# Another order of steps and loads in a chunked attention with a multiplicative feed-forward, and a last output block in four pieces

## The chip, the cores and the metric

The kernel runs on one core of a Trainium2 chip, in one launch. The metric is the device time of the core in microseconds (us). Five engines work side by side, each through its own list of instructions in order: TensorE (PE) multiplies, VectorE (DVE) and ScalarE (ACT) work on what it leaves in PSUM, GpSimd (POOL) issues the loads, and SyncE (SP) issues moves and stores.

## The reference

```python
q, k, v: (8, 8, 576, 64)          # batch, heads, sequence, head_dim
# chunks of 64 along the sequence, each chunk attends to itself alone
scores = q_c @ k_c.T / 8
attn   = softmax(scores)
out    = attn @ v_c
x      = out as (4608, 512)       # tokens x (heads * head_dim)
a = x @ w1; b = x @ w2            # 512 -> 1024
h = (a * b) @ w3                  # 1024 -> 1024
y = h @ w_out                     # 1024 -> 512, float32
```

All inputs are float32 in memory. The kernel works in bfloat16 and accumulates in float32.

## The kernel before, in words

The 4608 tokens are 18 *pairs* p = 0 to 17 of 256 tokens (four chunks with all eight heads); two pairs make one of nine *groups* g of 512 tokens. The two last products are folded: w3 @ w_out is computed once on the chip (`w3o`), so that each token is multiplied by w1, w2 and then by `w3o`.

Nothing is scheduled by loops. The string `ORDER` lists every step by a letter with its indices, and a loop at the end of `first_path` calls `do[letter](indices)`. The order of the steps in the string is the order of the instructions on each engine; between engines they run as their semaphores allow. The letters:

- Loads by POOL (queue q0, with a cast from float32 to bfloat16; one *block* is 256 KB as it lands): `q5`, `k5`, `v5` are q, k and v of pair 5 (each one block, in one to three DMAs); `i0` to `i3` are quarters of w1 and w2; `h0` and `h1` are the halves of w3 (four DMAs of one block each), `o` is w_out (four of one block). At most eight of POOL's DMAs are outstanding: each one's issue waits for the landing of the eighth before it. A q also waits until the transpose that read its buffer five pairs earlier is through, a v until the P that read its buffer six pairs earlier is.
- The first pair goes another way (`R`, `K`, and `D` for products with zeros while nothing else is there).
- `T5.0`, `T5.1` (DVE, L207): the 32x32 transposes of q and of k of pair 5. `G3.0`, `G3.1` (SP, four moves each): for pairs from 6 on, the transposed q and k of a group are moved to other partitions.
- `S5` (PE): scores; `E5` (ACT, L240): exponential; `P5` (PE): times v, with a column of ones for the sum. `N5.0`, `N5.1` (DVE, L269 and L272): reciprocal and normalization of the two halves of the tokens; each frees a PSUM buffer of P5.
- `X5.0`, `X5.1` (DVE, L305 or L313): transposes of the normalized x. `H3.0`, `H3.1` (SP, four moves each): the moves that follow for pairs from 6 on.
- `A6.2`, `B6.2` (PE): x times w1 and w2, a part of 128 (pairs below 4: 256) columns of d_ff; `C6.2` (ACT, L370) copies A's product from PSUM, `M6.2` (DVE, L387) multiplies it with B's. Pairs 0 to 3 go one by one; from pair 4 on, the steps of an even p cover a whole group of 512 tokens.
- `V0` to `V7` (DVE, L428): transposes of parts of w3; `W0` to `W3` (PE): w3 @ w_out; `Z0` to `Z3` (ACT): `w3o` from PSUM. W0 needs V0, V1 and all of w_out; V0 to V3 need h0, V4 to V7 need h1; W2 needs V4 and V5, W3 needs V6 and V7.
- `O5` (PE): the output of pair 5, from `w3o`; `Y5` (ACT, L417): from PSUM to SBUF; `Q5` (SP): its store, 512 KB.

All of PSUM is four buffers of two banks, and S, each half of P, A with B, W and O all take one. So a step of PE also waits for the reader of some earlier product: for an E, an N, an M, a Z or a Y. Which one is fixed when the program is built; the prediction names those that matter.

The last output, `O17`, goes in pieces, so that the copies and stores begin earlier: rows 0 to 127 in one piece of 512 columns, rows 128 to 255 in pieces of fewer columns, each with its own PSUM buffer, copy and store (L403 to L411).

Of the kernel before, what the change touches and what calls it, by code (L numbers as in the profile page):

```python
# [7 lines left out]

ORDER = """
R0.0 R1.0 R0.1 R1.1 v0 D0.0.1.9.512 K0.0 K1.0 T0.0.0 K0.1 T0.1.0 K1.1 S0.0 T0.0.1 E0.0 T0.1.1 q1 k1  # L10
S0.1 i0 E0.1 P0.0 T1.0 P0.1 D0.1.0.6.512 v1 N0.0 T1.1 N0.1 X0.0 X0.1 i1 S1 E1 D1.0.0.6.512 A0.0 B0.0
C0.0 i2 P1 q2 A0.1 B0.1 N1.0 k2 N1.1 C0.1 X1.0 i3 A0.2 C0.2 X1.1 A1.0 M0.0 M0.1 v2 q3 A1.1 B0.2 B1.0
B1.1 T2.0 k3 T2.1 v3 C1.0 M0.2 C1.1 S2 E2 q4 k4 A0.3 M1.0 M1.1 B0.3 P2 h0 o C0.3 M0.3 A1.2 N2.0 N2.1
X2.0 X2.1 T3.0 B1.2 A1.3 B1.3 C1.2 A2.0 C1.3 T3.1 C2.0 B2.0 M1.2 M1.3 S3 A2.1 E3 B2.1 P3 T4.0 M2.0
N3.0 C2.1 N3.1 A2.2 X3.0 C2.2 X3.1 B2.2 q5 h1 A2.3 B2.3 A3.0 M2.1 M2.2 v4 B3.0 A3.1 A3.2 V0 C2.3
M2.3 T4.1 C3.0 B3.1 k5 B3.2 V1 M3.0 W0 C3.1 q6 q7 k6 Z0 V2 q8 S4 V3 C3.2 k7 M3.1 W1 T5.0 v5 V4 E4 V5
V6 V7 W2 W3 T5.1 Z1 Z2 A3.3 T6.0 k8 q9 k9 Z3 M3.2 S5 T6.1 T7.0 q10 T7.1 E5 v6 v7 C3.3 P4 B3.3 N4.0
X4.0 M3.3 O0 G3.0 N4.1 k10 Y0 G3.1 T8.0 O1 X4.1 P5 T8.1 Y1 O2 Q0 N5.0 N5.1 X5.0 v8 X5.1 A4.0 S6 E6
T9.0 T9.1 S7 B4.0 T10.0 Y2 q11 O3 C4.0 M4.0 Q1 E7 P6 v9 N6.0 A4.1 N6.1 C4.1 Y3 B4.1 A4.2 X6.0 M4.1
G4.0 A4.3 X6.1 C4.2 P7 N7.0 C4.3 B4.2 G4.1 k11 B4.3 N7.1 X7.0 A4.4 M4.2 B4.4 Q2 M4.3 C4.4 T10.1 M4.4  # L20
A4.5 C4.5 S8 B4.5 A4.6 C4.6 A4.7 E8 B4.6 Q3 C4.7 X7.1 B4.7 M4.5 q12 P8 H3.0 M4.6 S9 H3.1 M4.7 O4 E9
T11.0 Y4 P9 N8.0 O5 k12 N8.1 A6.0 B6.0 Y5 T11.1 G5.0 T12.0 A6.1 X8.0 N9.0 B6.1 C6.0 C6.1 T12.1 A6.2
q13 X8.1 B6.2 N9.1 X9.0 M6.0 k13 C6.2 v10 T13.0 v11 X9.1 M6.1 A6.3 M6.2 q14 G5.1 C6.3 A6.4 q15 B6.3
C6.4 B6.4 A6.5 S10 C6.5 B6.5 T13.1 M6.3 M6.4 A6.6 H4.0 E10 P10 H4.1 M6.5 S11 N10.0 B6.6 k14 N10.1
v12 A6.7 C6.6 E11 G6.0 P11 M6.6 N11.0 B6.7 X10.0 N11.1 A8.0 A8.1 B8.0 G6.1 C6.7 C8.0 B8.1 A8.2 B8.2
C8.1 M6.7 T14.0 q16 A8.3 M8.0 C8.2 M8.1 X10.1 M8.2 X11.0 Q4 q17 T14.1 H5.0 B8.3 C8.3 S12 S13 X11.1
A8.4 E12 C8.4 B8.4 k15 H5.1 M8.3 E13 v13 k16 A8.5 B8.5 P12 M8.4 k17 v14 T15.0 N12.0 N12.1 O6 A8.6
v15 C8.5 C8.6 T15.1 Y6 T16.0 B8.6 A8.7 M8.5 C8.7 P13 Q5 M8.6 B8.7 X12.0 A10.0 C10.0 B10.0 N13.0
N13.1 M8.7 G7.0 A10.1 T16.1 C10.1 A10.2 X12.1 X13.0 M10.0 C10.2 G7.1 B10.1 B10.2 A10.3 B10.3 C10.3
M10.1 T17.0 A10.4 C10.4 M10.2 M10.3 A10.5 T17.1 B10.4 M10.4 X13.1 v16 H6.0 S14 C10.5 S15 G8.0 B10.5  # L30
M10.5 O7 G8.1 E14 E15 P14 A10.6 H6.1 N14.0 C10.6 B10.6 A10.7 N14.1 Q6 Y7 M10.6 P15 N15.0 N15.1 C10.7
X14.0 S16 B10.7 M10.7 O8 E16 Q7 A12.0 B12.0 C12.0 M12.0 Y8 A12.1 C12.1 P16 S17 N16.0 X14.1 B12.1 E17
A12.2 M12.1 B12.2 A12.3 C12.2 A12.4 B12.3 X15.0 B12.4 v17 C12.3 M12.2 A12.5 N16.1 B12.5 M12.3 H7.0
X15.1 A12.6 X16.0 A12.7 C12.4 M12.4 C12.5 M12.5 C12.6 P17 N17.0 Q8 B12.6 B12.7 M12.6 H7.1 A14.0
A14.1 C12.7 B14.0 N17.1 C14.0 M12.7 O9 B14.1 C14.1 Y9 A14.2 X16.1 M14.0 M14.1 C14.2 A14.3 B14.2 Q9
O10 B14.3 X17.0 H8.0 Y10 Q10 A14.4 C14.3 A14.5 X17.1 C14.4 B14.4 M14.2 B14.5 H8.1 M14.3 A14.6 O11
Y11 B14.6 M14.4 O12 C14.5 C14.6 Y12 A14.7 M14.5 A16.0 C14.7 C16.0 Q11 M14.6 B14.7 A16.1 C16.1 A16.2
B16.0 B16.1 M14.7 M16.0 C16.2 M16.1 Q12 A16.3 O13 B16.2 B16.3 A16.4 C16.3 M16.2 Y13 M16.3 C16.4
A16.5 A16.6 B16.4 A16.7 C16.5 B16.5 M16.4 O14 Y14 C16.6 B16.6 C16.7 M16.5 B16.7 M16.6 Q13 M16.7 O15
Y15 O16 Q14 Q15 Y16 Q16 O17  # L40
"""


# [5 lines left out]
def first_path(  # L49
# [11 lines left out]
    nc = tc.nc  # L61
    B, H, S, D = q.shape
    P = 128
# [5 lines left out]
    DM = H * D  # L69
# [22 lines left out]
    def inorder(ins):  # L92
        tc.keep_in_program_order(ins)
        return ins
# [7 lines left out]
    def psum(name):  # L102
        return ps.tile([P, 2, 512], f32, tag="p", name=name)
# [285 lines left out]
    def store(p, u0, u1, n0, n1, o_sb):  # L389
        move(out[p * PT + u0 * UT:p * PT + u1 * UT, n0:n1].rearrange("(u p) n -> p u n", p=UT), o_sb)  # L390

    def mm_o(dst, p, u, n0, n1):
        for ki in range(FO):
            t0 = p % 2 * PT + u * UT
            mm(dst, lhsT=ab_t[p // 2][:, ki, t0:t0 + UT],
               rhs=w3o[:, ki, n0:n1], start=(ki == 0), stop=(ki == FO - 1))

    def do_O(p):
        if p < NP - 1:
            ps_t[p] = psum("o_ps")  # L400
            for u in range(2):
                mm_o(ps_t[p][:, u, :], p, u, 0, DM)
            return  # L403

        o_sb = msb.tile([P, 2, DM], f32, tag="o_sb", name="o_sb")
        for u, n0, n1, copy in ((0, 0, DM, nc.scalar.copy), (1, 0, DM - P, nc.scalar.copy),
                                (1, DM - P, DM, nc.vector.tensor_copy)):
            t = psum("o_ps")
            mm_o(t[:, 0, 0:n1 - n0], p, u, n0, n1)
            inorder(copy(o_sb[:, u, n0:n1], t[:, 0, 0:n1 - n0]))  # L410
            store(p, u, u + 1, n0, n1, o_sb[:, u:u + 1, n0:n1])  # L411
# [42 lines left out]
    def load_half3(i):  # L454
# [10 lines left out]
    do = {"q": load_q, "k": load_k, "v": load_v, "i": load_w12, "o": load_wo, "h": load_half3, "T": do_T, "S": do_S, "R": do_R, "K": do_K, "E": do_E, "w": do_w, "x": do_x, "G": do_G, "H": do_H,  # L465
          "P": do_P, "N": do_N, "X": do_X, "A": do_A, "B": do_B, "C": do_C, "M": do_M, "D": do_D, "V": do_V,
          "W": do_W, "Z": do_Z, "O": do_O, "Y": do_Y, "Q": do_Q}
    for step in ORDER.split():
        do[step[0]](*(int(n) for n in step[1:].split(".") if n))
# [119 lines left out]
```

## Time and profile before

| | |
|---|---|
| median of 3 runs | 241.62 us (241.2 to 242.22) |
| the profiled execution | 242.34 us |
| its span (first to last instruction) | 240.8 us |
| mean granted TensorE clock | 0.993 |
| TensorE busy | 229.8 us (95%) |
| DVE, ACT, POOL busy | 152.5, 84.4, 83.4 us |
| DMA bytes | 39.21 MB, of them 18.88 on q0 (POOL's loads), 19.41 on q1 (SP's moves and stores) |

All step times below are from that one profiled execution, in us from the start of its span. The instructions of an engine stand in the trace in the order of the string, so each instruction belongs to a known step; a step's time is the start of its first instruction, and a landing is the time at which a DMA's completion reached its semaphore. Starts of some steps of TensorE: A0.0 15.20, P2 28.76, S3 34.95, B3.2 46.00, W0 48.05, S4 51.59, W1 52.23, W2 56.59, W3 60.05, O0 66.62, S6 78.70, O4 98.61, A6.0 105.99, A6.1 107.72, A6.2 109.45, O17 233.96. Landings: i3 25.94 and 27.73, k3 31.89, q4 35.63, k4 36.90, h0 42.33, w_out 47.92, h1 55.00, v4 55.92, k8 67.77, v8 91.01, k11 99.46, k12 103.17.

At the end of the span: O17's copies start at 235.93 (512 columns, ACT, 0.59), 237.19 (384, ACT, 0.48) and 237.69 (128, DVE, 0.29); SP issues its stores at 236.54, 237.69 and 238.13, and the last lands at 239.85.

### The profile page before, as it was taken

To read this page: it belongs to the slowest core of one execution; us is meant where nothing else is said; L and a number is where in the kernel's file an instruction comes from. 1 tells how busy PE (TensorE), PEld (TensorE's weight loads), DVE (VectorE), ACT (ScalarE), POOL (GpSimd) and SP (SyncE) were. 2 spreads that over 40 slices of the span, in tenths; PEclk is the share of its full clock that TensorE was granted. 3 is DMA by queue.
4 is the path that set the end of the run, shared out by engine and by line. 5 is a ranking of instruction groups with operands and counts; after the bars stand their busy time and mean duration, and the time that the engine had idled before them with its cause. 6 is when DMAs were issued, how large, how long until landed. Compare 5 with 4: busy or idle time off the path is not lost.

```text
span 240.8 us, 6221 instructions
## 1 busy us (share of the span) xinstructions
PE 229.8 (95%) x2621; PEld 119.3 (50%) x2621; DVE 152.5 (63%) x237; ACT 84.4 (35%) x119; POOL 83.4 (35%) x112
## 2 busy tenths in 40 slices
PE   6699999898999999999999999999999999999994
PEld 1367688743644444444444444454444444444442
DVE  2757799948996588898698898474774322223200
ACT  4323233141421543343536143355332223521322
POOL 7856866567864324576434510000000000000000
PEclk9799999999999999999999999999999999999999
DMA  6999999999999999999999997760410442202224
GB/s 176 179 185 188 178 175 199 197 187 179 173 203 210 257 215 268 213 196 214 214 230 218 213 264 126 175 221 4 131 44 7 131 131 87 90 0 88 83 92 174
DMA packets 94397, 39.21 MB, mean 163 GB/s; under 512 B 75296, under 2 KB 86816, under 8 KB 94368
## 3 DMA queue, kind: packets, MB, share of 16 engines
q0 software_dynamic: 82592, 18.88, 84.2%
q1 hardware_dynamic: 10720, 19.41, 26.8%
q10 hardware_dynamic: 1056, 0.52, 0.8%
q8 instruction: 20, 0.33, 0.5%
q14 instruction: 9, 0.07, 0.1%
HBM read 38.80 MB, written 9.44 MB: 200 GB/s over the span
## 4 chain that ended last, share of the span: by engine, by line
PE 75%; DMA 18%; POOL 3%; issue 1%; DVE 1%; ACT 0%; DVEq 0%; POOLq 0%
PE ab_ps L97 42%; PE o_ps L97 26%; DMA w<-in_moe_w_dram 12%; DMA wo<-in_moe_w_out_dram 3%; DMA qk<-in_q_dram 3%; PE w_ps L97 3%; PE pv L97 2%; PE s_ps L97 2%; POOL vbuf L100 2%; POOL w L100 1%; POOL qk L100 1%; DVE w3T L428 1%; DVE ab L387 0%; ACT o_sb L410 0%; DVE o_sb L410 0%
## 5 line engine op out<-in xcount | busy, mean ns | idle before, releaser
L97 PE MATMUL ab_ps<-xt,w 128*128 128x512 bf16 (+1 forms) x688 | 128.7, 342 | 0.4 <-DMA w<-in_moe_w_dram 0.3
L97 PEld LDWEIGHTS <-w 128*128 128x128 bf16 x704 | 67.0, 98 | 54.8 <-DMA w<-in_moe_w_dram 1.2
L387 DVE TENSOR_TENSOR ab<-a_sb,ab_ps 128x512 bf16<-128x512 f32 x71 | 47.2, 674 | 51.3 <-PE ab_ps L97 31.0
L370 ACT COPY a_sb<-ab_ps 128x512 f32<-128x512 f32 x71 | 41.4, 587 | 69.5 <-PE ab_ps L97 67.4
L97 PE MATMUL o_ps<-w3o,ab 128*128 128x512 bf16 (+2 forms) x296 | 64.7, 373 | 0.2 <-DVE ab L387 0.2
L207 DVE STREAM_TRANSPOSE qkT<-qk 128x1024 bf16<-128x1024 bf16 (+1 forms) x38 | 46.1, 1238 | 6.9 <-ACT qk L150 3.9
L97 PEld LDWEIGHTS <-ab 128*128 128x128 bf16 x296 | 28.4, 98 | 33.2 <-issue 0.7
L100 POOL DMA_DIRECT2D vbuf<-in_v_dram x40 | 33.9, 849 | 24.2 <-DMA vbuf<-in_v_dram 6.7
L417 ACT COPY o_sb<-o_ps 128x1024 f32<-128x1024 f32 x17 | 17.2, 1014 | 44.1 <-PE o_ps L97 43.4
L272 DVE TENSOR_TENSOR xn<-pv,rcs 128x512 bf16<-128x512 f32 x36 | 24.9, 692 | 1.2
L100 POOL DMA_DIRECT2D qk<-in_q_dram x23 | 17.9, 784 | 13.6 <-DMA w<-in_moe_w_dram 5.5
L240 ACT ACTIVATE e<-s_ps 128x1024 bf16<-128x1024 f32 (+1 forms) x17 | 16.9, 1001 | 14.4 <-PE s_ps L97 14.3
L100 POOL DMA_DIRECT2D qk<-in_k_dram x23 | 17.9, 781 | 11.4 <-DMA vbuf<-in_v_dram 4.0
L313 DVE STREAM_TRANSPOSE xm<-xn 128x512 bf16<-128x512 bf16 x24 | 16.3, 690 | 0.1
L97 PE MATMUL w_ps<-wo,w3T 128*128 128x512 bf16 x64 | 14.3, 379 | 1.7 <-DMA wo<-in_moe_w_out_dram 1.0
L291 POOL CROSS_LANE_REDUCE all_good<-good 128x1 f32<-128x1 f32 x1 | 0.4, 354 | 40.9 <-DVE both L289 40.9
L269 DVE RECIPROCAL rcs<-pv 128x8 f32<-128x8 f32 x36 | 7.0, 195 | 11.1 <-PE pv L97 11.0
L100 POOL DMA_DIRECT2D w<-in_moe_w_dram x16 | 11.1, 698 | 6.0 <-DMA w<-in_moe_w_dram 2.4
L428 DVE STREAM_TRANSPOSE w3T<-w 128x1024 bf16<-128x1024 bf16 x8 | 9.4, 1217 | 4.3 <-DMA w<-in_moe_w_dram 4.3
L97 PEld LDWEIGHTS <-e 64*32 64x32 bf16 (+1 forms) x768 | 7.5, 101 | 6.8 <-issue 4.2
L97 PEld LDWEIGHTS <-w3T 128*128 128x128 bf16 x64 | 6.0, 98 | 9.4 <-DVE ab L387 1.3
L97 PE MATMUL pv<-vbuf,e 64*32 64x65 bf16 (+1 forms) x768 | 10.1, 198 | 0.2
(28 smaller groups left out, 54.6 us busy)
## 6 DMA issues: line engine op xcount, KB each, us to landing
out_dram<-o_sb SPq DMA_DIRECT2D x17, 512.0 KB, 3.5
qkm<-qkT SPq DMA_DIRECT2D x48, 128.0 KB, 7.0
vbuf<-in_v_dram POOLq DMA_DIRECT2D x32, 128.0 KB, 10.2
w<-in_moe_w_dram POOLq DMA_DIRECT2D x16, 256.0 KB, 9.3
xt<-xm SPq DMA_DIRECT2D x48, 64.0 KB, 5.2
qk<-in_q_dram POOLq DMA_DIRECT2D x11, 256.0 KB, 10.4
qk<-in_k_dram POOLq DMA_DIRECT2D x11, 256.0 KB, 9.2
wo<-in_moe_w_out_dram POOLq DMA_DIRECT2D x4, 256.0 KB, 9.1
```

What stands on the lines that cost most here:

```text
L97: return inorder(nc.tensor.matmul(*a, **kw))
L100: return inorder(nc.gpsimd.dma_start(dst, src))
L207: inorder(nc.vector.transpose(qkT_t[g][:, :, p % 2, s, heads(h)].rearrange("p e h (y t) -> p h t e y", t=2), qk_t[p][:, s, heads(h)].rearr ...
L240: inorder(nc.scalar.activation(e_t[p][:, :, heads(hh)], s_t[p, hh][:].rearrange("p u (h q) -> p u h q", q=CH)[:, :, heads(hh)], Exp, scale ...
L269: inorder(nc.vector.reciprocal(rc, pv[:, :, :, D:W]))
L272: inorder(nc.vector.tensor_mul(xn_t[p][:, u], pv[:, :, :, 0:D], rc.to_broadcast([P, 2, 4, D])))
L291: inorder(nc.gpsimd.tensor_reduce(all_good[:], good[:], axis=mybir.AxisListType.C, op=op.add))
L313: inorder(nc.vector.transpose(xm_t[g][:, u, :, m].rearrange("p o (c y) -> p c o y", y=BL), xn_t[p][:].rearrange("p u r m d -> p (u r) m d" ...
L370: first[p, j] = inorder(nc.scalar.copy(a_t[p, j][:], ps_t[p, j][:, 0, :]))
L387: inorder(nc.vector.tensor_mul(o, view(a_t.pop((p, j))[:]), view(ps_t.pop((p, j))[:, 1, :])))
L417: inorder(nc.scalar.copy(o_sb[:], ps_t.pop(p)[:]))
L428: inorder(nc.vector.transpose(w3T_t[f][:].rearrange("p k (f y) -> p f k y", y=BL), w3[:, NB * f:NB * (f + 1), :].rearrange("p f (k x) -> p ...
```

## The change

The string `ORDER` is another one, with the same steps (each one once), and O17's second half goes in three pieces of 256, 128 and 128 columns instead of two of 384 and 128. The diff, with the string cut to the stretch in which the first steps and loads differ, and the code whole:

```diff
@@ ORDER
 R0.0 R1.0 R0.1 R1.1 v0 D0.0.1.9.512 K0.0 K1.0 T0.0.0 K0.1 T0.1.0 K1.1 S0.0 T0.0.1 E0.0 T0.1.1 q1 k1
-S0.1 i0 E0.1 P0.0 T1.0 P0.1 D0.1.0.6.512 v1 N0.0 T1.1 N0.1 X0.0 X0.1 i1 S1 E1 D1.0.0.6.512 A0.0 B0.0
-C0.0 i2 P1 q2 A0.1 B0.1 N1.0 k2 N1.1 C0.1 X1.0 i3 A0.2 C0.2 X1.1 A1.0 M0.0 M0.1 v2 q3 A1.1 B0.2 B1.0
-B1.1 T2.0 k3 T2.1 v3 C1.0 M0.2 C1.1 S2 E2 q4 k4 A0.3 M1.0 M1.1 B0.3 P2 h0 o C0.3 M0.3 A1.2 N2.0 N2.1
-X2.0 X2.1 T3.0 B1.2 A1.3 B1.3 C1.2 A2.0 C1.3 T3.1 C2.0 B2.0 M1.2 M1.3 S3 A2.1 E3 B2.1 P3 T4.0 M2.0
-N3.0 C2.1 N3.1 A2.2 X3.0 C2.2 X3.1 B2.2 q5 h1 A2.3 B2.3 A3.0 M2.1 M2.2 v4 B3.0 A3.1 A3.2 V0 C2.3
-M2.3 T4.1 C3.0 B3.1 k5 B3.2 V1 M3.0 W0 C3.1 q6 q7 k6 Z0 V2 q8 S4 V3 C3.2 k7 M3.1 W1 T5.0 v5 V4 E4 V5
-V6 V7 W2 W3 T5.1 Z1 Z2 A3.3 T6.0 k8 q9 k9 Z3 M3.2 S5 T6.1 T7.0 q10 T7.1 E5 v6 v7 C3.3 P4 B3.3 N4.0
+S0.1 i0 E0.1 P0.0 P0.1 T1.0 D0.1.0.6.512 v1 N0.0 T1.1 N0.1 X0.0 X0.1 i1 i2 S1 E1 D1.0.0.6.512 A0.0
+C0.0 P1 B0.0 q2 N1.0 k2 N1.1 i3 X1.0 X1.1 A0.1 C0.1 v2 M0.0 B0.1 A0.2 M0.1 q3 k3 A1.0 C0.2 B0.2 M0.2
+B1.0 C1.0 A1.1 T2.0 T2.1 B1.1 A0.3 M1.0 C1.1 S2 B0.3 C0.3 M1.1 E2 P2 M0.3 N2.0 N2.1 q4 A1.2 A1.3
+B1.2 C1.2 B1.3 X2.0 X2.1 A2.0 C1.3 T3.0 B2.0 T3.1 M1.2 T4.0 C2.0 v3 S3 h0 M1.3 M2.0 o q5 A2.1 E3 k4
+B2.1 P3 N3.0 h1 X3.0 A2.2 N3.1 X3.1 C2.1 B2.2 A2.3 C2.2 B2.3 k5 A3.0 M2.1 M2.2 C2.3 V0 q6 C3.0 A3.1
+V1 C3.1 q7 B3.0 A3.2 M2.3 C3.2 B3.1 k6 M3.0 B3.2 M3.1 V2 W0 T4.1 T5.0 S4 v4 M3.2 V3 V4 Z0 A3.3 k7 W1
+C3.3 V5 T5.1 v5 V6 T6.0 q8 q9 W2 Z1 V7 S5 T6.1 E4 T7.0 T7.1 W3 G3.0 B3.3 Z2 M3.3 P4 E5 k8 Z3 N4.0 O0
...
@@ do_O
-        for u, n0, n1, copy in ((0, 0, DM, nc.scalar.copy), (1, 0, DM - P, nc.scalar.copy),
-                                (1, DM - P, DM, nc.vector.tensor_copy)):
+        for u, n0, n1, copy in ((0, 0, DM, nc.scalar.copy), (1, 0, DM // 2, nc.vector.tensor_copy),
+                                (1, DM // 2, DM - P, nc.scalar.copy), (1, DM - P, DM, nc.vector.tensor_copy)):
```

Since each engine takes its own steps alone, the string is easiest to read engine by engine. The stretches of which the prediction speaks, before and after:

```
POOL before  k3 v3 q4 k4 h0 o q5 h1 v4 k5 q6 q7 k6 q8 k7 v5 k8 q9 k9 q10 v6 v7 k10 v8 q11 v9 k11 q12 k12 q13 k13 v10
POOL after   k3 q4 v3 h0 o q5 k4 h1 k5 q6 q7 k6 v4 k7 v5 q8 q9 k8 k9 q10 v6 v7 k10 q11 q12 v8 v9 k11 v10 k12 q13 v11
PE before    B3.1 B3.2 W0 S4 W1 W2 W3 A3.3 S5 P4 B3.3 O0 O1 P5 O2 A4.0 S6 S7 B4.0 O3 P6
PE after     B3.1 B3.2 W0 S4 A3.3 W1 W2 S5 W3 B3.3 P4 O0 P5 O1 A4.0 B4.0 O2 S6 S7 O3 P6
PE before    B4.7 P8 S9 O4 P9 O5 A6.0 B6.0 A6.1 B6.1 A6.2 B6.2
PE after     B4.7 S9 P8 O4 P9 O5 A6.0 B6.0 A6.1 A6.2 B6.1 B6.2
DVE before   V1 M3.0 V2 V3 M3.1 T5.0 V4 V5 V6 V7 T5.1 T6.0 M3.2 T6.1 T7.0 T7.1
DVE after    V1 M2.3 M3.0 M3.1 V2 T4.1 T5.0 M3.2 V3 V4 V5 T5.1 V6 T6.0 V7 T6.1 T7.0 T7.1
DVE before   T11.0 N8.0 N8.1 T11.1 T12.0 X8.0 N9.0 T12.1 X8.1 N9.1 X9.0 M6.0
DVE after    T11.0 N8.0 N8.1 T11.1 T12.0 T12.1 N9.0 X8.0 X8.1 N9.1 X9.0 M6.0
SP before    Q0 Q1 G4.0 G4.1 Q2 Q3 H3.0 H3.1 G5.0
SP after     Q0 Q1 G4.0 G4.1 Q2 H3.0 H3.1 Q3 G5.0
```

In the second half, the outputs O6 to O9 come earlier among the products than before (O8 behind B10.2, where it was behind B10.7), and S12 to S17 with P12 to P17 stand among other products.

## The prediction

> **What bounds the kernel now.** I read the page's engine shares first, then the chain that ended last, the waits of TensorE, TensorE's timeline in the weight stage, and the two DMA queues by stretches. The page says that TensorE is the engine to look at:
>
> ```profile
> PE 229.8 (95%) x2621; PEld 119.3 (50%) x2621; DVE 152.5 (63%) x237; ACT 84.4 (35%) x119; POOL 83.4 (35%) x112
> ...
> PE   6699999898999999999999999999999999999994
> ...
> DMA  6999999999999999999999997760410442202224
> ```
>
> PE is idle for 11.0 us of 240.8, nearly all in the first quarter and the last slice; the DMA engines are full until about 155 us. So an order can win only what TensorE still waits for, and it can lose anywhere, since nothing else is slack behind it. The chain in the weight stage, and the same stretch on TensorE:
>
> ```profile
> 35.55 7.99 DMA wo<-in_moe_w_out_dram
> 43.54 0.83 issue
> 44.37 10.62 DMA w<-in_moe_w_dram
> ...
> 55.29 1.26 DVE w3T L428
> ...
> 56.59 7.08 PE w_ps L97 x32
> ```
>
> ```profile
> 38.13 8.91 PE L97 MATMUL ab_ps<-xt,w 128*128 128x256 bf16 x80
> 48.05 3.61 PE L97 MATMUL w_ps<-wo,w3T 128*128 128x512 bf16 x16 [1.02 <-DMA wo<-in_moe_w_out_dram]
> 51.59 0.71 PE L97 MATMUL s_ps<-qkT 32*64 32x64 bf16 x64
> 52.23 3.63 PE L97 MATMUL w_ps<-wo,w3T 128*128 128x512 bf16 x16
> 56.59 7.08 PE L97 MATMUL w_ps<-wo,w3T 128*128 128x512 bf16 x32 [0.73 <-DVE w3T L428]
> ```
>
> Two waits stand there: W0 starts at 48.05, 1.18 after the pace of the products before it (B3.2 at 46.00 plus 0.87), because the last piece of w_out lands at 47.92; W2 starts at 56.59, 0.90 late, because the second half of w3 lands at 55.00 and V4 takes 1.26. From 56.59 TensorE never stops for long: against the usual distance of the starts (0.87 for an A or B, 3.46 for an O or W, 0.38 for an S or P from the sixth pair on) four waits remain, 0.17 (S6 to S7), 0.14 (before O3), 0.26 (before O4) and 0.35 (at S16).
>
> The queues: q0 carries POOL's loads, q1 SP's moves and stores.
>
> ```profile
> q0 software_dynamic: 2728, 0.35, 91.0%
> q1 hardware_dynamic: 343, 0.90, 66.3%
> ```
>
> That is 72 to 78 us: q0 moves 0.35 MB in 6 us, while from 60 to 66, alone, it moves 1.04. The price of a load follows. Alone, eight blocks of 256 KB (k5 to k8, v4's landing at 55.92 to k8's at 67.77) take 1.48 us each. From h1's landing (55.00) to k12's (103.17) 21 blocks land: 31.1 us of their own, so 17.1 us went to the 4.7 MB that q1 moved meanwhile (G3, G4, four stores, H3), 3.6 us per MB.
>
> **Part by part.** *Up to P2 (28.8 us) nothing changes.* POOL's queue is the same up to k3, and TensorE there waits for i1, i2 and i3. P1 goes one step earlier, S2 one later; A0.3 and B0.3 then wait for i3's landings (25.94 and 27.73), so B0.3 starts at 27.78 as before. S3 still follows T3.1 (ends 34.89). Sum 0.
>
> *Weights.* Behind k3 the queue was v3 q4 k4 h0 o q5 h1; now it is q4 v3 h0 o q5 k4 h1. h0 and o are ahead of one block more, k4, which took 1.27 (35.63 to 36.90): w_out's last piece lands at 46.65, and W0 starts when the products end, 46.9. h1 has the same bytes ahead of it as before, so it still lands at about 55.0, V4 still ends at 56.5, and W2 still starts at 56.6. The gain of W0 is kept only as far as other work fills the time up to W2. The work moved in front of W2 is A3.3, 0.87, of which I keep 0.80 when the row durations behind W2 are added up. What eats the rest: k4 lands at about 49.3 (o at 46.65, then q5 and k4 at 1.3 each), so T4.1 ends at 50.7 and S4 starts there instead of 50.45; then T5.0 and M3.2 are queued on DVE behind T4.1, and W1 needs M3.2's buffer: 52.5 against 52.25. Both small waits lie ahead of the wait for h1 and cost nothing. Behind W2, T5.1 and T6.0 now stand between V5, V6 and V7 on DVE; V7 ends at 62.35, and the second half of W3 wants it at 62.5. O0 then starts at 65.8 instead of 66.62: **-0.80**.
>
> *Short waits.* S6 and S7 need G3, which SP issues behind T7.1, now at 66.0 instead of 66.44: -0.17. O3 no longer stands behind Y2's buffer: -0.14. M4.7 to O4 keeps 0.18 of 0.26: -0.08. G8 is issued behind T17.1 well ahead of S16, which now stands behind O9: -0.35. Together **-0.74**. The other regroupings of S, P, A, B and O carry the same instructions and as many changes of kind (18), so 0; the buffers that they wait for (an M, N, E or Y each) are ready 0.3 us or more before by the same row durations.
>
> *The new wait.* POOL's later order is k10 q11 q12 v8 v9 k11 v10 k12; it was k10 v8 q11 v9 k11 q12 k12. So k12 has 22 blocks behind h1 instead of 21: 55.0 + 22 x 1.48 + 17.1 = 104.7, against 103.17. And DVE's order was T11.1 T12.0 X8.0 N9.0 T12.1 X8.1 N9.1; it is T11.1 T12.0 T12.1 N9.0 X8.0 X8.1 N9.1. T12.0 ends at 103.0, T12.1 stands waiting for k12, and behind it on DVE wait N9.0, which frees the buffer of A6.1, and N9.1, which frees A6.2's. With the rows below, T12.1 takes 104.75 to 106.0, N9.0 ends at 106.9, X8.0 and X8.1 take 0.6 each, N9.1 ends at 108.95.
>
> ```profile
> 104.31 0.17 DVE L269 RECIPROCAL rcs<-pv 128x8 f32<-128x8 f32 x1
> 104.51 0.69 DVE L272 TENSOR_TENSOR xn<-pv,rcs 128x512 bf16<-128x512 f32 x1
> 105.12 1.31 DVE L207 STREAM_TRANSPOSE qkT<-qk 128x1024 bf16<-128x1024 bf16 x1
> 106.33 0.66 DVE L313 STREAM_TRANSPOSE xm<-xn 128x512 bf16<-128x512 bf16 x1
> ```
>
> TensorE would be at A6.1 at 106.5 and at A6.2 at 107.4: it waits 0.4 and then 1.2, **+1.6** together. A wait costs nothing while k12 lands by 103.2, and a microsecond for each one later. In the trace of before T12.1 waits for nothing, so this is an estimate from landings; its ends are 0 (k12 at 103.2) and +3.5 (below), and I take 1.6, which is nearest to the counted blocks.
>
> The clock could make a wait dearer. In the rows of 42 to 48 and 54 to 60 us TensorE is short of work for about 1 us and the granted clock stays 1.00. The Trainium skill ("TensorE: Matmul & The Clock Gate", "What's actually happening") lets the clock fall only after an idle window of about 3.4 us; by it too a wait of this size adds nothing, while one twice as long could.
>
> *The last block.* TensorE's columns of O17 are the same (512, then 384 as 256 and 128, then 128), so its end does not move. Before, ACT copies 384 columns in 0.48, DVE 128 in 0.29, and SP issues the last store at 238.13, which lands 1.72 later. Now DVE copies 256 in about 0.4 (between 0.29 for 128 and 0.67 for 512 on the L387 row), ACT 128 in about 0.27, DVE the last 128 at the same 237.69. SP's three issues of 0.44 each start at 237.25, so the last goes out at 238.15. The bytes ahead of it are out a little sooner. **+0.05**, between -0.2 and +0.3.
>
> **Sum**: -0.80 - 0.74 + 1.6 + 0.05 = +0.1 us on the profiled execution (span 240.8, 242.34 with what lies around it). That execution is 0.7 above the median of the runs, which I take as offset: 241.62 + 0.1 = 241.7. About 0.5%, or 1.2 us, is what a measurement of this kernel can tell from no change.
>
> **The rivals.** *The full gain* (faster): k12 lands by 103.3, because q1's price per MB is lower when Q3 is no longer issued at 87 but behind H3, at 96. For it: that store's 0.5 MB then meets fewer moves. Against it: it still lies ahead of k12. Then only -1.54 + 0.05 is left: 240.1. Chance 0.27.
>
> *k12 meets G5* (slower). SP issues G5.0 as soon as T11.1 ends, at 101.8, 0.9 earlier than before, and G3's first bytes flowed 3 us behind their issue (66.44; none on q1 up to 69). If k12 is not in by 104.8, its rest shares the engines with G5: half a block, 0.13 MB, at the 0.06 MB per us of 72 to 78 takes 2.2 instead of 0.75. With that 1.45 and a lag of 0.5 ahead of it k12 lands at 106.6, and the wait is 3.5 instead of 1.6: 243.6. It begins with a lag of 0.1 us, and passes the 0.5% bound with k12 at 105.8. For it: the small margin; against it: 102 to 105 shows q0 with 0.51 MB and q1 with almost nothing. Chance 0.26. The Trainium skill ("DMA: Bandwidth & Descriptors", "Queues, rings and completion order") has each DMA engine alternate between queues by packets; it fits the rows of 72 to 78, and by it G5's large packets take most of the engine once they flow.
>
> *The weights are not won*: W2 waits longer because h1's last piece is gated by o's third landing plus the 0.83 of issue seen at 43.54, and lands at 55.8 instead of 55.0. Then O0 is back at 66.6, and the time 242.5. Against it: seven pieces are outstanding, so the queue does not run dry. Chance 0.07.
>
> **How the numbers follow.** The forecast (k12 between 103.7 and 105.4, 241.0 to 242.4) has 0.40. The cases below 240.4 are the full gain; those above 242.8 are G5's. Faster 0.27, same 0.47, slower 0.26. The range reaches from 239.9 (full gain with the tail's -0.2) to 243.6 (G5). The forecast's own range is 241.0 to 242.4.
>
> **What would show it.** Right: W0 at 46.9 without a wait, W2 still behind V4 at 56.6, O0 near 65.8; T12.1 idle before it with q or k as releaser near 103 to 104.7; a wait of ab_ps on DVE's xn near 107 to 109; O17's last store landing 5.9 us (within 0.2) behind O17's first product, as before. Wrong: no idle on DVE before T12.1 (then the full gain), a wait at P8 for v8 (I have it at 94 against 96.9), at A8.0 for H4, which X9.0 issues later (0.6 of margin), or one of more than 0.3 us elsewhere behind 110 us.

## The result, and the profile after

| | before | after |
|---|---|---|
| median, 20 runs each on one chip | 242.14 us (241.20 to 242.65) | 242.69 us (241.96 to 243.76) |
| ratio to before | | 1.003, 95% interval 1.0019 to 1.0040 |
| profiled execution / its span | 242.34 / 240.8 us | 242.95 / 241.4 us |

After is slower by 0.7 us (0.5 to 1.0), inside what was called no change. As a number, 242.69 lies above the forecast's own range (241.0 to 242.4) and inside the whole one (239.9 to 243.6); 0.5 of the distance to 241.7 is the base, which was 241.62 in three runs and is 242.14 in twenty. The sum had +0.1; the profiled spans differ by +0.6. The shares and slices of the page after:

```profile
PE 228.1 (94%) x2608; PEld 119.1 (49%) x2629; DVE 153.4 (64%) x238; ACT 84.5 (35%) x119; POOL 83.4 (35%) x112
...
PE   6699989999999999979999999999999999999994
...
DMA  6999999999999999999999999580232004320224
```

The two 8s of before on PE, in the eighth and tenth slice (42 to 48 and 54 to 60 us), have become 9s; an 8 stands in the sixth (30 to 36) and a 7 in the eighteenth (103 to 109), where before had 9s. (21 of TensorE's 2629 matmul records are missing here, so below the starts of its steps come from its weight loads, up to 0.2 ahead of the matmul row.) TensorE's timeline in the weight stage:

```profile
38.77 8.91 PE L97 MATMUL ab_ps<-xt,w 128*128 128x256 bf16 x80
47.51 3.62 PE L97 MATMUL w_ps<-wo,w3T 128*128 128x512 bf16 x15
51.06 0.71 PE L97 MATMUL s_ps<-qkT 32*64 32x64 bf16 x64
51.70 1.05 PE L97 MATMUL ab_ps<-xt,w 128*128 128x256 bf16 x8
52.58 7.07 PE L97 MATMUL w_ps<-wo,w3T 128*128 128x512 bf16 x31
```

No row ends in a bracket: W0 follows the products at once, A3.3 (51.70) fills the place in front of W1, and W1 runs into W2. Both waits of before are gone, and O0 starts at 65.28 instead of 66.52. The time comes back at 105 us, as the chain of what ended last has it:

```profile
94.87 9.94 DMA qk<-in_k_dram
104.81 0.02 issue
104.84 1.32 DVE qkT L207
106.15 0.08 DVE rcs L269
...
106.26 0.69 DVE xn L272
106.95 1.21 DVE xm L313 x2
108.16 0.10 DVE rcs L269
...
108.29 0.70 DVE xn L272
108.99 0.05 issue
109.04 7.08 PE ab_ps L97 x32
```

k12 lands at 104.81, T12.1 is released by it, N9.0 ends at 106.95 and N9.1 at 108.99. On DVE (first) and TensorE (second):

```profile
100.47 2.49 DVE L207 STREAM_TRANSPOSE qkT<-qk 128x1024 bf16<-128x1024 bf16 x2 [0.77 <-DMA qk<-in_k_dram]
104.84 1.32 DVE L207 STREAM_TRANSPOSE qkT<-qk 128x1024 bf16<-128x1024 bf16 x1 [1.88 <-DMA qk<-in_k_dram]
```

```profile
104.27 1.89 PE L97 MATMUL ab_ps<-xt,w 128*128 128x512 bf16 x8
107.01 1.04 PE L97 MATMUL ab_ps<-xt,w 128*128 128x512 bf16 x4 [0.85 <-DVE xn L272]
109.04 3.20 PE L97 MATMUL ab_ps<-xt,w 128*128 128x512 bf16 x14 [0.99 <-DVE xn L272]
```

DVE stands 1.88 us with N9.0 and N9.1 queued behind T12.1; TensorE loses 1.22 and 1.16 against its pace, 2.4 together (the brackets count only the idle part). In the windows of 104 to 108 and 108 to 112 us the granted clock is 1.00, so these waits cost no more than themselves. The Trainium skill ("TensorE: Matmul & The Clock Gate", "What's actually happening") lets the clock fall only after an idle window of about 3.4 us; the trace agrees, as far as waits of 1 us can. By it a wait of twice 1.6 us would still be too short, other than the prediction has it.

At the end O17 starts 0.19 later than before (233.94 against 233.75), the last store lands 0.19 later (240.04 against 239.85), but the span ends 0.62 later. After the last issue SP looks at its DMA semaphores one by one, in a fixed order, 0.06 us each. From the two traces:

```
                           before           after
last store's semaphore     119 (last)       110 (seven more behind it)
its landing                239.85           240.04
SP passes 113              238.81           240.18 (110 at 240.06, 111 at 240.12)
SP passes 118, 119         239.58, 239.87   240.42, 240.48
end of the span            240.78           241.40
end behind the landing     0.93             1.36
```

The stores take eight semaphores in turn. With one store more the last one of the kernel falls on 110, the first of these eight that SP looks at, and the walk over the other seven (0.42 us) comes behind the last landing instead of ahead of it.

### The profile page after: what moved, and what is told of

The parts are those of the page before. It is cut to its first block, busy times and chain, and to the rows that moved or that the text cites. A ratio compares the mean times of both kernels' runs of the same rounds, so it can differ in the third digit from the quotient of the medians.

```text
span 241.4 us, 6230 instructions
## 1 busy us (share of the span) xinstructions
PE 228.1 (94%) x2608; PEld 119.1 (49%) x2629; DVE 153.4 (64%) x238; ACT 84.5 (35%) x119; POOL 83.4 (35%) x112
## 4 chain that ended last, share of the span: by engine, by line
PE 80%; DMA 11%; POOL 3%; DVE 2%; issue 1%; ACT 0%; POOLq 0%
PE ab_ps L97 47%; PE o_ps L97 23%; DMA w<-in_moe_w_dram 7%; PE w_ps L97 6%; DMA qk<-in_k_dram 4%; PE pv L97 3%; PE s_ps L97 3%; POOL vbuf L100 2%; POOL qk L100 1%; POOL w L100 1%; DVE xn L272 1%; DVE qkT L207 1%; DVE xm L313 1%; ACT e L240 0%; DVE o_sb L410 0%
```

## The experiments

Theory: the order wins in the weight stage and loses it at T12.1; the fourth store adds 0.4 at the end. Each ratio is to runs of before on the same chip; "lost" is a start against the pace of the prediction. In the diffs steps stand as on their engine, and the pieces of O17's second half as columns and engine of the copy.

**Last block alone.**

```diff
 ORDER of before
-0 to 384 ACT, 384 to 512 DVE
+0 to 256 DVE, 256 to 384 ACT, 384 to 512 DVE
```

> The order of before with the last block of after (512, 256, 128, 128 columns). Theory (two parts: the order costs about 0.2, and the fourth store 0.4 more, because SP at the end waits for its eight DMA semaphores one by one in a fixed order and the fourth store's is the third in that order): 0.4 us slower than before; the last store lands within 0.1 of 239.85, and the span ends 0.5 behind that landing instead of 0.1. Rival (the smaller pieces cost nothing, and all of the 0.7 us that lies between the two kernels is the order's): the same time as before, span 240.8.

Ratio 1.0017 (0.9999 to 1.0035), +0.4 us: the size expected, though the interval just reaches no change. In its trace the span ends 1.35 behind the last landing, where before had 0.93: the difference is the one expected, though the expectation's 0.1 and 0.5 left out the 0.85 or so that follows in both. Its trace of before's order shows something else too: w_out lands at 47.40 and h1 at 54.23 (in the profiled execution of before 47.92 and 55.00), W0 loses only 0.52 and W2 0.65, O0 starts at 65.75.

**Order alone.**

```diff
 ORDER of after
-0 to 256 DVE, 256 to 384 ACT, 384 to 512 DVE
+0 to 384 ACT, 384 to 512 DVE
```

> The order of after with the last block of before (512, 384, 128 columns). Theory (two parts): 0.4 us faster than after, and 0.1 to 0.3 slower than before; T12.1 still waits for k12 (about 104.8), A6.1 and A6.2 still lose about 2.4 us together, O0 starts near 65.3. Rival (all of it is the order's): as slow as after. Beside it: the 0.66 us that TensorE stands still inside S3 in the trace of after; if it belongs to the list of instructions it is there again behind the 56th product of S3, if it was chance it isn't.

Ratio 1.0022 (0.9999 to 1.0044), +0.5 us, more than expected, and by the ratios 0.2 below after instead of 0.4; with the 0.4 above it makes 0.9, against after's 0.7 (0.5 to 1.0). The intervals are too wide to tell these apart. T12.1 starts at 104.67 and A6.1 with A6.2 loses 2.0. In its trace the span ends 0.4 sooner behind O17's start than in after (7.04 against 7.46). TensorE stands still for 0.66 inside S3 again. Of the ten kernels below six show the same stop (0.16 to 0.44 idle, one of them with TensorE's order of before) and four don't. So it belongs to that place, not to the change; its cause is open. One thing stands beside it in the traces: in all eight that stop, the 57th product starts 1.5 to 1.7 us behind the end of a 16 KB packet on q8, the queue that the page lists as `instruction`. That TensorE waits there for its own instructions is not shown, since in before the same product started 1.3 us behind such a packet without a stop.

**T12.1 behind N9.1.**

```diff
-T12.0 T12.1 N9.0 X8.0 X8.1 N9.1
+T12.0 N9.0 X8.0 X8.1 N9.1 T12.1
```

> After, with the one step T12.1 moved behind N9.1 on DVE, so that N9.0, X8.0, X8.1 and N9.1 no longer stand behind the wait for k12. Theory (the wait for k12 ahead of N9.0 and N9.1 is what eats the gain of the weight stage): A6.1 and A6.2 lose at most 0.3 us instead of 2.4, TensorE stays about 2.1 ahead to the end, and the time is 2.1 us below after. Rival (the gain is given back further on, since the loads, not TensorE, set the pace until 155 us: DVE then has T12.1 ahead of M6.0, and A8.0 wants H4): the wait comes back behind A6.2, and the time is 0 to 1 us below after.

Ratio 0.9967 (0.9948 to 0.9986): 0.8 us faster than before and, by the ratios, 1.5 faster than after; between theory and rival. TensorE in its trace, where no row between 103 and 122 us has a bracket:

```profile
104.20 9.66 PE L97 MATMUL ab_ps<-xt,w 128*128 128x512 bf16 x44
113.79 0.45 PE L97 MATMUL s_ps<-qkm 64*64 64x64 bf16 x32
```

The wait at A6.1 and A6.2 is gone, and this profiled execution (240.70 us; median 241.28) is 2.3 below after's. The usual execution keeps 1.5 of it; where the rest stays is seen in the next kernel and in the last two.

**k12 ahead of v10** (T12.1 where after has it).

```diff
-POOL  k11 v10 k12 q13
+POOL  k11 k12 v10 q13
```

> After, with k12 issued ahead of v10 on POOL's queue, and T12.1 left ahead of N9.0. Theory: k12 has one block less ahead of it and lands about 1.4 us earlier, near 103.4; T12.1 ends near 104.7, N9.1 near 107.5; A6.1 and A6.2 lose about 1.0 instead of 2.4, and the time is 1.4 us below after. v10 lands at about 104.8, long before P10 at 120. Rival (k12's landing is set by what SP's queue moves meanwhile, not by the blocks ahead of it): k12 lands within 0.4 of 104.8, and the time is that of after.

Ratio 0.9979 (0.9958 to 0.9999): 1.2 us below after. k12 lands at 102.89, 1.9 earlier; A6.1 loses nothing and A6.2 0.60. But S10 then loses 0.4 (G5's last move lands at 114.18), and A8.0 0.68: it starts at 120.69, and H4.1's last move lands at 120.58. The gain meets two further waits.

**Q3 behind H4.1** (and a third buffer for the outputs).

```diff
-SP  H3.1 Q3 G5.0 G5.1 H4.0 H4.1 G6.0
+SP  H3.1 G5.0 G5.1 H4.0 H4.1 Q3 G6.0
```

> After, with the store Q3 moved behind H4.1 on SP, and a third buffer for the outputs, so that Y5 does not wait for it; T12.1 stays ahead of N9.0. Theory (what SP's queue moves ahead of k12 delays k12, 3.6 us per MB): 0.52 MB less lie ahead of k12, which lands up to 1.9 us earlier, near 103.0; A6.1 and A6.2 lose at most 0.7 us together instead of 2.4; G5 and H4 come earlier too, so that A8.0 doesn't wait for H4.1 either; the time is 1.5 to 2.0 us below after. Rival (k12's landing is set by the 22 blocks on its own queue, whatever SP moves): k12 lands at 104.3 or later and the time is that of after.

Ratio 1.0003 (0.9982 to 1.0025): 0.65 below after, less than half of the 1.5 to 2.0 expected. The first half of the theory holds: T12.1 is released at 103.35 instead of 104.84, 1.5 for 0.52 MB or 2.9 us per MB, and A6.1 and A6.2 lose 1.0. The second half does not (this kernel's lines are five lower than after's):

```profile
107.55 7.08 PE L92 MATMUL ab_ps<-xt,w 128*128 128x512 bf16 x32 [0.62 <-DVE xn L267]
...
116.01 0.67 PE L92 MATMUL s_ps<-qkm 64*64 64x64 bf16 x31 [1.24 <-DMA qkm<-qkT]
```

S10 waits for G5, whose last move lands at 115.88 (after: 113.65), though its first four moves were issued at the same time (102.01 against 101.86; the other four from 105.08, 0.8 later) and Q3 no longer stands ahead of it. A8.0 still loses 0.3 behind H4.1. POOL's k13 lands at 108.64 and 110.33, over 3 us earlier than in after: what the store left free went to the loads that follow. That it is these loads which slow G5 is argued, not shown: G5 took 13.9 us from its first issue (102.01) to its last landing, and 11.8 in after. The Trainium skill ("DMA: Bandwidth & Descriptors", "Queues, rings and completion order") has each DMA engine switch between queues packet by packet, by which a move gets only its turns while POOL's queue is full; the trace agrees as far as this goes. The traced execution took 243.47; five of the twelve lie at 241.2 to 241.8, so this late G5 need not be in each of them.

**Both, with the last block of before.** The order of the kernel with T12.1 late, Q3 behind H4.1, three pieces.

> The order of after with T12.1 behind N9.1 and with Q3 behind H4.1 (third output buffer), and the last block of before (512, 384, 128). Theory: the wait at A6.1 and A6.2 is gone, A8.0 has a margin of over 1 us on H4.1, and the end comes 0.1 behind the last landing instead of 0.5: 2.1 + 0.4 us below after, about 1.8 below before. Rival (what the kernel with T12.1 late alone fell short of its trace, 1.5 by the times against 2.3, is scatter and not a wait for H4.1): then Q3's move adds nothing, and it is 0.4 us below that kernel, 1.1 to 1.3 below before.

Ratio 0.9987 (0.9965 to 1.0009). Neither expectation holds. Set against the kernel "T12.1 late, with the last block of before" below (0.9970), from which it differs by Q3's place and the third buffer alone, Q3's move brings nothing; by the middle values it costs 0.4, but the intervals overlap. H4.1 lands at 119.94, A8.0 is due at 119.67 and starts at 120.15.

**The last store on the last semaphore.**

```diff
-            store(p, 0, 2, 0, DM, o_t.pop(p)[:])
+            o_sb = o_t.pop(p)
+            if 9 <= p <= 15:
+                for u in range(2):
+                    store(p, u, u + 1, 0, DM, o_sb[:, u:u + 1, :])
+            else:
+                store(p, 0, 2, 0, DM, o_sb[:])
```

> After, with each of the stores Q9 to Q15 issued in two halves (seven DMAs more on SP, at a time when the queues are nearly idle), so that the last store of O17 uses the last one of the eight semaphores in SP's order at the end, and not the third. Theory (0.06 us for each semaphore that SP still has to look at behind the last landing): the last store lands at the same distance behind O17's first product as in after, and the span ends 0.1 behind that landing instead of 0.5: 0.4 us below after. Rival (the end behind the last landing is a fixed cost of the fourth piece): the time is that of after.

Q9 to Q15 go as two stores of 128 rows each, instead of one of 256. Ratio 1.0006 (0.9993 to 1.0019), 0.6 us below after. In its trace (an execution of 244.05, the slowest of its thirteen, so only the end is read) the store lands at 241.56, SP passes 118 and 119 at 241.11 and 241.57, and the span ends at 242.49: 0.93 behind the landing, as before, with four pieces. In all traces that show the landing, the distance is 0.93 where the last store has semaphore 119 (four kernels beside before) and 1.36 where it has 110 (six kernels, after among them). So the 0.43 is the semaphore's place, not the pieces.

**A3.3 back behind W3, with T12.1 late.**

```diff
-PE  W0 S4 A3.3 W1 W2 S5 W3
+PE  W0 S4 W1 W2 S5 W3 A3.3
```

> After with T12.1 behind N9.1 (as in the kernel of that name) and with A3.3 and C3.3 moved back behind W3. Theory (the weight stage gains only as much as work is put ahead of W2): W2 is reached 0.87 us earlier, still has to wait for V4 near 55.7, and O0 and all that follows come 0.6 to 0.9 us later than in the kernel with T12.1 late. Rival (the gain is w_out's earlier landing, and A3.3's place doesn't matter): O0 stays within 0.2.

Ratio 1.0029 (1.0012 to 1.0046), 1.5 us above the kernel with T12.1 late. O0 starts at 66.85 instead of 65.16, 1.7 later, where 0.6 to 0.9 was expected. The two places on TensorE (lines five lower again):

```profile
55.85 3.63 PE L92 MATMUL w_ps<-wo,w3T 128*128 128x512 bf16 x16 [0.74 <-DVE w3T L423]
...
66.14 0.79 PE L92 MATMUL pv<-vbuf,e 64*32 64x65 bf16 x64 [0.71 <-ACT w3o L436]
```

W2 waits for V4, loses 1.1 and starts at 55.85, as in the kernel with A3.3 ahead of it, so A3.3's 0.87 comes on top: that much is as the theory wants. The other 0.8 is a wait inside P4 that the edit makes, since one of its PSUM buffers is now freed by a Z. So about half of the 1.5 us says what A3.3's place is worth.

**A3.3 back, with T12.1 as in after.**

> After with A3.3 and C3.3 moved back behind W3, and T12.1 left where after has it, ahead of N9.0. Theory (as long as T12.1 waits there for k12, whose landing the queues set, the weight stage's gain is worth next to nothing): O0 comes 1.7 us later than in after, as in the pair of kernels with T12.1 late, but T12.1 still starts near 104.8, A6.1 near 107 and A6.2 near 109; the losses there shrink from 2.4 to about 0.7, and the time is that of after within 0.4 us. Rival (the gain counts whatever stands behind it): 1.5 us above after, as the same move cost with T12.1 late.

Ratio 1.0023 (1.0005 to 1.0041): 0.2 below after, so here the same 1.6 us in the weight stage is worth nothing, as the theory has it. The trace gets there in another way than expected: with TensorE 1.6 later at O0 (66.89), k12 lands at 103.20, T12.1 starts at 103.83 without a wait, A6.2 at 108.47, and A8.0 then loses 0.63 (121.78, 0.10 behind H4.1's last landing). The moves and stores of SP's queue follow TensorE and DVE and were issued later (H3.1 at 94.42 instead of 92.61, Q3 at 97.57 instead of 95.94), so they may have taken less of the time ahead of k12. How much of the 1.6 between the two landings of k12 is this and how much scatter stays open: with T12.1 late and the same edit it landed at 104.22.

**k4 later in the order of before.**

```diff
-POOL  q4 k4 h0 o q5 h1        DVE  T4.1 V1 M3.0 V2
+POOL  q4 h0 o q5 k4 h1        DVE  V1 M3.0 V2 T4.1
```

> Before with k4 moved behind q5 on POOL's queue, and its transpose T4.1 moved behind V2 on DVE, so that it doesn't hold up V1. Theory (w_out's earlier landing alone is worth nothing: W2 waits for h1 and V4 all the same): w_out's last piece lands near 46.4, W0 starts without a wait, W2 waits longer by as much and starts near 55.8, O0 is within 0.3 of the 65.75 of the order of before in the run with the new tail alone, and the time is that of before within 0.3 us. Rival (each wait that goes is a gain): 0.5 to 1.2 us below before.

Ratio 1.0028 (1.0008 to 1.0048): 0.7 us slower than before, so no gain; no change within 0.3 was expected. Its trace is as expected:

```profile
47.13 3.62 PE L97 MATMUL w_ps<-wo,w3T 128*128 128x512 bf16 x15
...
55.69 7.08 PE L97 MATMUL w_ps<-wo,w3T 128*128 128x512 bf16 x32 [0.40 <-DVE w3T L428]
```

w_out lands at 46.06, W0 starts at 47.02 without a wait, W2 loses 0.93 instead and starts at 55.69, O0 at 65.62 (65.75 in the first experiment). W0's wait has become W2's. That trace shows no cost (its execution, 241.73, is the fastest of twelve), so where the 0.7 us of the others goes is open; 0.4 of it lies in the spans (median 240.7 against 240.3).

**T12.1 late, with the last block of before.**

> The order of after with T12.1 behind N9.1, and the last block of before (512, 384, 128 columns). Theory: the gain of the kernel with T12.1 late (1.5 us below after, 0.8 below before) and the 0.4 of the semaphores at the end add up: 1.2 us below before. A8.0, which would be reached near 119.2, waits for the last move of H4.1 in some executions (that landing lay between 118.8 and 120.6 in the traces with T12.1 late or k12 early), so not all of the 2.1 arrives. Rival (the first run of T12.1 late was lucky, and the moves take the gain back): 0.4 below before at most.

Ratio 0.9970 (0.9946 to 0.9994): 0.7 us faster than before, where 1.2 was expected, and 1.3 faster than the same last block with after's order. The 0.4 of the semaphores does not show beside the kernel with four pieces (0.9967); the intervals of about 0.5 us to each side are too wide for it. But this trace, unlike the first one of T12.1 late, shows where a part of the rest of the 2 us stays:

```profile
104.28 9.66 PE L97 MATMUL ab_ps<-xt,w 128*128 128x512 bf16 x44
...
118.76 1.04 PE L97 MATMUL ab_ps<-xt,w 128*128 128x512 bf16 x4
120.24 1.02 PE L97 MATMUL ab_ps<-xt,w 128*128 128x512 bf16 x4 [0.45 <-DVE xn L272]
```

A6.1 and A6.2 lose nothing; A8.0 loses 0.59. The bracket names xn, since N10.1 ended just before, at 120.16; but as the program is built A8.0 waits for N10.0 (ended at 119.31) and for the moves of H4, and H4.1's last move lands at 120.10. In five traces that show both, A8.0 starts 0.11 to 0.21 behind that landing (k12 early, Q3 late twice, A3.3 back with T12.1 late, and this one). In after it lands at 120.44 and A8.0 is due at 121.35, so it had 0.9 to spare, less than the 2.1 by which TensorE came forward. In the first trace of T12.1 late the last update of H4.1 comes at 119.10 and A8.0 starts at 119.20, just as it is due.

**O6 and P11 ahead of A8.0.** The kernel before this, with work put in front of A8.0.

```diff
-PE  B6.7 A8.0 P11 B8.0 A8.1 ... S12 S13 O6 P12
+PE  B6.7 O6 P11 A8.0 B8.0 A8.1 ... S12 S13 P12
```

> The kernel with T12.1 late and the last block of before, with O6 and then P11 put ahead of A8.0 on TensorE (O6 stood 16 us later; Y6 follows it on ACT, and the outputs have a third buffer), so that A8.0 is reached about 3.8 us later and H4.1 has landed by then. Theory (what the kernel with T12.1 late gives back, it gives back at A8.0, which waits for the last move of H4.1): the 0.5 to 0.6 us that A8.0 lost are gone, no wait of more than 0.3 takes their place up to 150 us, and the span is 0.5 us below that of the kernel without O6's move (its runs: 239.55 median), so 1.2 us below before by the spans. Rival (the moves and loads set the pace further on too): the same wait comes back at S12 for G6 or at A10.0 for H5, and the time is that of the kernel without O6's move.

Ratio 1.0069 (1.0044 to 1.0094): slower by 1.7 us. A8.0's loss is gone, as the theory has it, but neither it nor the rival saw what O6 had been doing in its old place:

```profile
134.31 0.71 PE L97 MATMUL s_ps<-qkm 64*64 64x64 bf16 x64
135.89 0.45 PE L97 MATMUL pv<-vbuf,e 64*64 64x65 bf16 x32 [0.88 <-ACT e L240]
136.81 1.89 PE L97 MATMUL ab_ps<-xt,w 128*128 128x512 bf16 x8 [0.47 <-ACT e L240]
```

It covered the two exponentials of S12 and S13. P12 now waits for E12, A8.6 for E13's buffer, and by A10.0 2.2 us are lost. About 0.3 of it is what the rival named: A10.0 starts at 144.82, and H5.1's last move lands at 144.76.

The fastest kernels of the study, faster than before and after, are the two with T12.1 late: 241.28 and 241.25 us, where before had 241.93 and 241.88 on the same chips.

## Why the prediction was right, step by step

*Up to P2: 0.* Right: P2 at 28.83 (28.76 before), S3 behind T3.1 at 34.80. The stop inside S3 that then cost 0.64 was not in the sum and is not the change's.

*Weights, -0.80.* The sign and the mechanism were right, the size was taken against the wrong execution. w_out landed at 46.22 (46.65 in the sum), k4 at 48.70 (49.3), W1 started at 52.48 (52.5). But h1, which the sum left at 55.0, landed at 54.09, V4 ended at 55.62 and W2 started at 55.82 without a wait, 0.8 earlier than the sum had it; O0 came at 65.28 instead of 65.8. Against the profiled execution of before that is -1.24. But 55.00 was a late landing of that one execution: the two other kernels with the rest of before's order (the last block alone, k4 later, with the same loads ahead of h1) have it at 54.23 and 54.10, and those with after's order at 54.09 to 54.83 (in three of them read from V4's start, 0.29 behind it). Against the last block alone, with O0 at 65.75, the gain is 0.47, or 0.94 from A2.1 on, behind S3's stop. The step that failed is "h1 still lands at about 55.0" as a property of the order. That k4's move is worth something only with work put ahead of W2 was seen from both sides: k4 alone gained nothing, and A3.3 back cost 1.5 us, of which about half is its place ahead of W2 and half a wait inside P4 that this edit makes.

*Short waits, -0.74.* Right in sign and slightly too small: between O0 and O4 -0.51 against the execution of before (-0.39 in the sum), and about -0.4 at S16 (-0.35).

*The new wait, +1.6.* The mechanism was right step by step: k12 104.81 (104.7), T12.0's end 102.96 (103.0), T12.1's end 106.15 (106.0), N9.0's end 106.95 (106.9), N9.1's 108.99 (108.95). Its size was 2.4, because TensorE would have been there at 105.8 and 106.7 instead of the 106.5 and 107.4 of the sum: what the weights gained more, this wait took. The two kernels with T12.1 late show that it is the eater of the gain: 1.5 and 1.3 us come back when the one step moves. The two with A3.3 back show it the other way round: with O0 1.6 to 1.7 later, the time is 1.5 us longer where T12.1 doesn't stand in front, and no longer where it does.

*The last block, +0.05.* Right as far as the sum went: the last store lands 6.10 behind O17's start, as before. Wrong in what was left out: the sum ended at the landing, and the semaphore of the fourth store added 0.43 behind it.

*The sum.* Against the first experiment's trace of the order of before: -0.47 (weights with S3's stop), -0.58 (O0 to O4), +2.38, -0.47 (S16) make +0.86, and O17 starts 0.86 later (233.94 against 233.08). The last term is what the others leave; the waits at S16 make 0.42 of it. The two spans lie only 0.46 apart (241.40 and 240.94), since in that experiment the last store landed 6.51 behind O17's start instead of 6.10. That the forecast was near is in part luck, since three errors were small and of both signs: a gain read too large or too small according to the execution it is set against, a wait read too small, and an end left out.

*The rivals.* The full gain needed k12 by 103.3; it came at 104.81. What it would be worth was overrated: 240.1 in the prediction is 1.5 below before, and the kernels without the wait reach 0.7 to 0.8 below. A part of the difference is A8.0 and H4, which the prediction named with "0.6 of margin" as a sign of error and priced at nothing: 0.59 in the trace of one of the two kernels, nothing in that of the other. How the rest divides is not shown. k12 meeting G5 did not happen in after: k12 landed where the counted blocks put it, and G5's first move at 108.69; that G5 can be late was seen at S10 with Q3 moved. The price of 3.6 us per MB of SP's queue was 2.9 there.

## What to carry to other kernels

When the loads are full, a wait that goes can come back at the next step that stands close behind a landing: list those margins (here k12 at T12.1, H4.1 at A8.0, v8 at P8 with 0.24) before counting a gain, and count it only up to the smallest. A step that waits for a load belongs behind everything on its engine that others need soon; moving T12.1 by four steps is what made the new order pay. And a single profiled execution is one draw: a landing that the sum rests on should be seen in more than one trace.

## What was not expected of the hardware

SP's look at the semaphores at the end of the program takes 0.06 us each in a fixed order, and the last store's place in that order moved the end by 0.43 us (0.93 or 1.36 behind the landing, with no value in between). A place in TensorE's list, the 57th product of S3, stopped it for 0.16 to 0.66 us in 8 of the 14 traces with no releaser in the profile. And executions with the same loads ahead of h1 had its landing 0.9 us apart (54.09 to 55.00).
